# Up weights whose last 64 rows come as two loads of one column half each, with small loads moved in SyncE's order

## The chip, the core and the metric

The kernel runs on one core of one Trainium2 chip. The metric is the device time of one execution in microseconds (us). A profiled execution has a span of its own (first to last instruction) and a time of its own.

## The reference

Three stages follow one another; the result has 3072 rows of 320.

```python
# 1: mLSTM over 4 batches, 8 heads, 768 steps, head size 40
C = f_stab * C + i_stab * outer(v_t, k_t);  n = f_stab * n + i_stab * k_t
y_t = sigmoid(o_t) * (C @ q_t) / max(|n . q_t|, 1)
x = y.transpose(0, 2, 1, 3).reshape(3072, 320)
# 2: soft mixture of 8 experts, 4 slots each
logits = x @ phi                                  # phi: 320 x 32
slot_input = softmax(logits, 0).T @ x             # 32 x 320
slot_out[e] = relu(slot_input[e] @ w1[e]) @ w2[e] # w1: 320 x 1024, w2: 1024 x 320, 8 experts
x = softmax(logits, 1) @ slot_out
# 3: second mixture, weights w1, w2 of its own, gate 320 x 8
P = exp(x @ w_gate - max), then 8 rounds of row and column normalisation
out = sum over e of P[:, e:e+1] * (relu(x @ w1[e]) @ w2[e])
```

## The kernel before

**Stage 1** works through 24 chunks of 128 time steps (`NT` = 24). `step(i)` handles chunk i and prepares chunks i+1 and i+2; its parts are run in the order that the string `ORDER` (for i = 0: `ORDER0`) gives. The names that matter here: `KT`/`QT` transpose k and q of chunk i+2 on TensorE (`ptk`, L379); `E0`/`E1` compute the decay of chunk i+2 on TensorE (`pe`, L398) out of the rows `R`, which come from DRAM for two chunks at a time; `V` is `pv` (L473), the product with the values of chunk i. SyncE (SP) issues all loads but two, in program order, because TensorE, ScalarE, SP, VectorE and GpSimd follow the order written by hand in this part:

- `DK` (`load_kq`, L151) loads k and q of chunk i+5 into one of three buffers, `DV` (`load_v`, L156) the values of chunk i+2 into one of three, `O` (`load_o`, L161) the output gates some chunks ahead, each load of 128 rows of 8 pieces of 40 numbers.
- `R` (`load_R`, L334) loads the rows for two later chunks, in every second step.
- `W` (`load_w`, L672) takes the next `WN[i]` pieces of the weights of stage 2 from the generator `ahead_parts`.
- `load_small` loads `phi` (three loads) and the gate weights of stage 3 (`wg_sb`, three loads by `load_k`, L121), once, ahead of step 0. `lg_p` reads `phi_sb` first in step 5; `wg_sb` is read only after the last expert of stage 2.

`end()` does the last two chunks, in the order of `END`; its entry `sl20` sends what `ahead_parts` still has.

**Weights.** Every weight matrix has 320 x 1024 or 1024 x 320 numbers (1280 KB) and takes one slot in SBUF. There are 15 slots. Slots 0 to 10 are filled by `ahead_parts`; the others (`wb`) only after stage 1 has given its memory back, and the first ones are used again for the weights of the last expert and the first of stage 3. An up weight (`w1_parts`) is sent in pieces: two of 128 rows of 1024 numbers (512 KB each), and the last 64 rows, which lie in the slot as two blocks of 64 partitions, one for each half of the columns:

```python
yield v[:, 4, :], src[e, 256:320, :].rearrange("p (a f) -> a p f", a=2)
```

The destination of this piece is 128 partitions of 512 numbers; the source has the dimensions 2 (column half), 64 (row), 512 (column). A down weight (`w2_parts`) is sent in two pieces of 640 KB.

**Stage 2** runs expert by expert: `up_t(e)` transposes (`pth`, L1035), `up(e + 1)` multiplies with the up weight (`pu`, L1010 for the first 256 rows and L1016 for the last 64), `down(e)` with the down weight (`pd`, L1046). After the last expert, `s1_p(0)` multiplies with the first up weight of stage 3 (again `pu`, L1010 and L1016; its slot is `big`).

**Stage 3** is the long one: for each of 8 experts and 6 blocks of 512 rows, `g1` computes the hidden values (`z`, L1269) and `g2` the products (`y`, L1290 to L1292). Up weights of later experts are loaded by `load_m2w`, also through `w1_parts`.

Of the kernel before, what the change touches and what calls it, by code (L numbers as in the profile page):

```python
# [20 lines left out]
def mlstm_moe_kernel(  # L21
# [16 lines left out]
    nc = tc.nc  # L38
    B, H, S, D = q.shape
    N, DM = out.shape  # L40
    E, _, F = m2_w1.shape
# [9 lines left out]
    KT = [(0, 112), (112, 112), (224, 96)]  # L51
# [10 lines left out]
    NXR = 13  # L62
    NBIG = 3
    ORDER = (
        "LF' STm PK R DV O W CS E0 E0a E0g YC' Yg' KT KTa QT QTa X Xa E1 E1a E1g G0 DK LT LV I ST UM STd CB V US LP LD G LA S"
        " W0 W1 YB"
    )
    ORDER0 = "O KT KTa QT E0 E0a QTa E0g ST STd PC PK V E1 E1a E1g G0 DK CB DP US S W0 W1 YB"
# [50 lines left out]
    def load_k(eng, dst, src):  # L119
        for kt, (o, n) in enumerate(KS):  # L120
            eng.dma_start(out=dst[0:n, kt, :], in_=src[o:o + n, :])  # L121
# [31 lines left out]
    def load_v(i):  # L153
        b, c = divmod(i, NCH)
        sl = slice(c * L, (c + 1) * L)
        nc.sync.dma_start(out=vz[i % NV][:, :, 0:D], in_=v[b, :, sl, :].rearrange("h p d -> p h d"))  # L156

    def load_o(i0, i1):
        for i in range(i0, i1):
            b, c = divmod(i, NCH)  # L160
            nc.sync.dma_start(  # L161
                out=xs_(i).rearrange("p (h d) -> p h d", h=H),
                in_=o_gate[b, :, c * L:(c + 1) * L, :].rearrange("h p d -> p h d"),
            )
# [17 lines left out]
    O0 = 3  # L182
# [107 lines left out]
    def load_csa():  # L290
        for a in range(3):
            nc.sync.dma_start(
                out=csa[a * BH:(a + 1) * BH, :].rearrange("r (g s) -> r g s", g=SG),
                in_=cpd.rearrange("(g r) a s -> r g a s", g=SG)[:, :, a, :],
            )
# [35 lines left out]
    def load_R(p):  # L331
        b, c = divmod(p * CPS, NCH)
        r0 = c // CPS * BH + b * H
        nc.sync.dma_start(out=Rt[p % 2][96:99, :, :], in_=gpd[r0:r0 + H, :, :].rearrange("r a s -> a r s"))  # L334
# [21 lines left out]
    def load_small():  # L356
        for kt in range(NKT - 1):
            nc.sync.dma_start(out=phi_sb[:, kt, :], in_=phi[KT[kt][0]:KT[kt][0] + 112, :])
        nc.sync.dma_start(out=phi_sb[16:112, NKT - 1, :], in_=phi[224:320, :])
        load_k(nc.sync, wg_sb, m2_wg)  # L360

    Cst = [mid.tile([P, JP, D1], F32, name=f"C_{j}", bufs=1) for j in range(2)]
    Cbd = [mid.tile([P, JP, 2, D1], F32, name=f"Cb_{j}", bufs=1) for j in range(2)]
# [73 lines left out]
    def st_p(i):  # L437
        for j in range(JP):
            for r in range(2):
                nc.tensor.matmul(  # L440
                    o_c[DP * r:DP * r + D, j, :], kp[i % PD][:, 2 * j + r, :], vz[i % NV][:, 2 * j + r, :],
                    start=True, stop=True, tile_position=(0, DP * r),
                )

    def st_m(i):
        if i % NCH:
            Cds[i] = mid.tile([P, JP, D1], F32, tag="Cd", name="Cd")
            nc.gpsimd.tensor_tensor(
                out=Cds[i], in0=Cst[(i % NCH - 1) % 2], in1=dec[:, :, i:i + 1].to_broadcast([P, JP, D1]),
                op=ALU.mult,  # L450
            )

    def st_d(i):
        Cn = Cst[i % NCH % 2]
        if i % NCH:
            nc.vector.tensor_tensor(out=Cn, in0=o_c, in1=Cds.pop(i), op=ALU.add)
        else:
            nc.vector.tensor_copy(Cn, o_c)
# [199 lines left out]
    def w1_parts(dst, src, e):  # L658
        v = dst.rearrange("p (a f) -> p a f", f=F // 2)
        for t in range(2):  # L660
            yield v[:, 2 * t:2 * t + 2, :].rearrange("p a f -> p (a f)"), src[e, t * P:(t + 1) * P, :]
        yield v[:, 4, :], src[e, 256:320, :].rearrange("p (a f) -> a p f", a=2)

    def w2_parts(dst, src, e):
        v = dst.rearrange("p (k d) -> p k d", d=DM)
# [4 lines left out]
    def load_w(parts):  # L670
        for d, s_ in parts:
            nc.sync.dma_start(out=d, in_=s_)  # L672
# [26 lines left out]
    ahead_parts = ahead()  # L699

    def step(i):
        b, c = divmod(i, NCH)
        n, s1 = i + 2, i + 1
        T, S1 = n < NT, s1 < NT
        X = i >= 2
        gq, j = divmod(i - 2, 4)
        if j < 3:
            gq -= 1
        if gq < 0:
            j = 9  # L710
        C_ = c < NCH - 1
        nxt = b + 1 < B

        ops = dict(
            KT=lambda: T and k_p(n, 0), KTa=lambda: T and k_a(n, 0),
            QT=lambda: T and k_p(n, 1), QTa=lambda: T and k_a(n, 1),
            E0=lambda: T and e_p(n, 0), E0a=lambda: T and e_a(n, 0), E0g=lambda: T and e_g(n, 0),
            E1=lambda: T and e_p(n, 1), E1a=lambda: T and e_a(n, 1), E1g=lambda: T and e_g(n, 1),
            ST=lambda: C_ and st_p(i), STm=lambda: C_ and st_m(i), STd=lambda: C_ and st_d(i), CB=lambda: C_ and st_b(i),
            S=lambda: S1 and s_p(s1), W0=lambda: S1 and s_d(s1, 0), W1=lambda: S1 and s_d(s1, 1),  # L720
            PK=lambda: T and pr_k(n),
            V=lambda: pv(i), I=lambda: c and p_st(i),
            X=lambda: X and x_p(i - 2), Xa=lambda: X and x_a(i - 2),
            Yg=lambda: i in nqs and y_g(i),
            UM=lambda: c and y_u(i), US=lambda: y_a(i), YB=lambda: i < NT - 3 and y_b(i), YC=lambda: i in ysrc and y_c(i),
            G=lambda: i in SIG and sig_o(*SIG[i]),
            G0=lambda: i or sig_o(0, 1), PC=lambda: put_csl(1), DP=decays_p,
            CS=lambda: i % HC == 1 and i + 5 < NT and put_csl((i + 5) // HC),
            LT=lambda: j == 1 and lt_p(gq), LV=lambda: j == 1 and lt_v(gq),
            LP=lambda: j in (2, 3) and (sl_p, lg_p)[j - 2](gq),  # L730
            LD=lambda: j in (1, 2, 3) and (lt_d, sl_d, lg_d)[j - 1](gq),
            LA=lambda: j in (1, 3) and (lt_a, lg_e)[j // 2](gq),
            LF=lambda: j == 1 and lt_f(gq),
            O=lambda: load_o(*LO[i]),
            R=lambda: i and i % CPS == 0 and i + 4 < NT and load_R((i + 4) // CPS),
            W=lambda: load_w(islice(ahead_parts, WN[i])),
            DV=lambda: T and i and load_v(n),
            DK=lambda: i + 5 < NT and load_kq(i + 5),
        )
        for o in (ORDER if i else ORDER0).split():  # L740
            if o.endswith("'"):
                if last:
                    last[-1][o[:-1]]()
            else:
                ops[o]()
        last[:] = [ops]
# [19 lines left out]
    load_o(0, 1)  # L766
    load_R(1)
    load_v(2)
    load_csa()
    load_o(1, 2)  # L770
    e_g(0, 0)
    pr_k(0)
    e_g(0, 1)
# [10 lines left out]
    put_csl(0, SW)  # L784
    masks()
    decays_d()
    load_small()
    load_w(islice(ahead_parts, 1))
    load_o(2, O0)
    load_kq(4)  # L790
    load_R(2)
    load_o(O0, O0 + 1)
    load_w(islice(ahead_parts, 1))
    nc.gpsimd.memset(xr[:, :, DM:DM + 1], 1.0)
# [6 lines left out]
    SIG = {s: (s + 2, s + 3) for s in range(4, 22)} | {1: (1, 2), 2: (2, 4), 3: (4, 6)}  # L801
    OL = [4, 5, 6, 7] + list(range(8, NT)) + [NT] * NT
    LO = {i: (OL[i], OL[i + 1]) for i in range(NT + 1)}
    WN = [0, 1] * 8 + [1, 1, 2, 2, 3, 3]
    for i in range(NT - 2):
        step(i)
    def end():
        n0, n1, n2, n3 = range(NT - 4, NT)
        wide = lambda t: t.rearrange("p a l -> p (a l)")[:, 0:H * D1].rearrange("p (h d) -> p h d", h=H)
        ux, ov = {}, {}  # L810

        def own(key):
            ov[key] = wide(ps_s.tile([P, 4, L], F32, tag="s", name=key))
            return ov[key]

        def u_(i):
            ux[i] = wide(pre.tile([P, 4, L], F32, tag="dd", name="ux", bufs=6))
            u_m(i, ux[i], ov.get("st", o_st) if i == n3 else o_st)

        def r_(i):  # L820
            u_s(i, ux[i], ov["in"] if i == n3 else o_in)
            ysrc[i] = ux[i]

        todo = dict(
            st=lambda: (st_m(n2), st_p(n2)), sl20=lambda: load_w(ahead_parts), d20=lambda: (st_d(n2), st_b(n2)),
            s23=lambda: s_p(n3, ((ps_e, "e"), (ps_t, "t"))), w0=lambda: s_d(n3, 0), w1=lambda: s_d(n3, 1),
            lt4=lambda: lt_p(gl - 1), tv4=lambda: lt_v(gl - 1), q4=lambda: sl_p(gl - 1), e4=lambda: sl_d(gl - 1),
            i22=lambda: p_st(n2), v22=lambda: pv(n2), i23=lambda: p_st(n3, own("st")), v23=lambda: pv(n3, own("in")),
            y21=lambda: y_c(n1, nc.gpsimd), y22=lambda: y_c(n2, nc.gpsimd), y23=lambda: y_c(n3),
        )  # L830
        for j, i in enumerate((n0, n1, n2, n3)):
            todo[f"x{20 + j}"] = lambda i=i: x_p(i)
            todo[f"a{20 + j}"] = lambda i=i: x_a(i)
            todo[f"u{20 + j}"] = lambda i=i: u_(i)
            todo[f"r{20 + j}"] = lambda i=i: r_(i)
            todo[f"n{20 + j}"] = lambda i=i: y_b(i)
            todo[f"g{20 + j}"] = lambda i=i: y_g(i)
        for o in END.split():
            todo[o]()
# [662 lines left out]
```

## Time and profile before

| | us |
|---|---|
| median of 3 runs | 956.61 (955.43 to 956.73) |
| profiled execution, its own time | 954.06 |
| its span | 952.3 |
| TensorE busy in the span | 909.3 |
| VectorE / ScalarE / GpSimd busy | 571.0 / 359.0 / 95.3 |

TensorE is busy for 95% of the span. Of the chain of work that ended last, 89% of the span is TensorE and 7% DMA. The granted TensorE clock, as a mean over the span, is 0.976 of full speed. The span has three parts: stage 1 to about 156 us, stage 2 to about 219 us, stage 3 from there to the end.

### The profile page before, as it was taken

The page shows a single profiled execution, that of the slowest core. Times are in us where ns is not written, and L with a number is a line of the kernel's source. Part 1 is how long each engine was busy: PE and PEld are TensorE (multiplying, and loading weights), DVE is VectorE, ACT ScalarE, POOL GpSimd, SP SyncE. Part 2 cuts the span into 40 slices and gives each one's busy share as a digit, 9 for nine tenths or more (in the row PEclk, how much of TensorE's full clock was granted, in tenths as well). Part 3 has the DMA queues.
Part 4 walks back from the last instruction along what each step waited for, and adds up shares of the span by engine and source line. Part 5 has one row for each costly group of instructions (what it writes and reads, how often), then busy time and mean ns, then how long its engine had stood idle before and what let it go on. Part 6 is the DMA issues. An engine that isn't in the chain of part 4 may idle for free.

```text
span 952.3 us, 18828 instructions
## 1 busy us (share of the span) xinstructions
PE 909.3 (95%) x7972; PEld 628.9 (66%) x7972; DVE 571.0 (60%) x1168; ACT 359.0 (38%) x701; POOL 95.3 (10%) x194
## 2 busy tenths in 40 slices
PE   8799977858999999999999999999999999999998
PEld 5688865424667666666666666666666666666665
DVE  7477845614689768575557456645745565544543
ACT  6455642315334335243433244224424343423221
POOL 5566652000000000000000000000000000000000
PEclk9899987969999999999999999999999999999999
DMA  6898988864021003010101011001100000000111
GB/s 125 171 205 155 210 191 242 240 205 135 1 63 36 14 1 112 1 56 1 56 2 56 1 57 50 7 17 40 56 1 1 1 1 1 1 1 29 49 42 49
DMA packets 128973, 63.85 MB, mean 67 GB/s; under 512 B 102425, under 2 KB 122649, under 8 KB 128889
## 3 DMA queue, kind: packets, MB, share of 16 engines
q1 hardware_dynamic: 128617, 62.16, 25.3%
q8 instruction: 62, 1.02, 0.4%
q10 hardware_dynamic: 272, 0.49, 0.2%
q14 instruction: 22, 0.18, 0.1%
HBM read 58.20 MB, written 4.23 MB: 66 GB/s over the span
## 4 chain that ended last, share of the span: by engine, by line
PE 89%; DMA 7%; DVE 2%; SPq 1%; ACT 1%; issue 0%; POOL 0%; ACTq 0%; DVEq 0%
PE y L1290 22%; PE y L1292 22%; PE y L1291 22%; PE z L1269 9%; PE ptk L379 2%; PE pss L428 2%; PE oa L473 2%; DMA wb<-in_moe_w_dram 2%; DMA big<-in_moe_w_dram 2%; PE pe L398 1%; DMA kq<-in_k_dram 1%; PE ob L484 1%; DMA vz<-in_v_dram 1%; PE ptx L548 1%; DMA R<-gpd 1%; SPq L672 1%
## 5 line engine op out<-in xcount | busy, mean ns | idle before, releaser
L1290 PE MATMUL y<-wx,hh 128*128 128x320 f16 x1344 | 402.1, 299 | 0.0
L1292 PE MATMUL y<-wx,hl 128*128 128x320 f16 x1344 | 401.7, 299 | 0.0
L1291 PE MATMUL y<-wx,hh 128*128 128x320 f16 x1344 | 401.6, 299 | 0.0
L1272 ACT ACTIVATE hh<-z 128x512 f16<-128x512 f32 x384 | 209.4, 594 | 431.5 <-PE z L1269 430.9
L1273 DVE SCALAR_TENSOR_TENSOR hl<-z,hh 128x512 f16<-128x512 f32 x384 | 248.4, 686 | 52.9 <-ACT hh L1272 52.4
L1305 DVE SCALAR_TENSOR_TENSOR acc<-y,Ps,acc 128x320 f32<-128x320 f32 x168 | 92.4, 550 | 209.9 <-PE y L1292 209.5
L1290 PEld LDWEIGHTS <-hh 128*128 128x128 f16 x1536 | 150.5, 98 | 73.2 <-ACT hh L1272 0.5
L1291 PEld LDWEIGHTS <-hh 128*128 128x128 f16 x1536 | 150.4, 98 | 73.2
L1292 PEld LDWEIGHTS <-hl 128*128 128x128 f16 x1536 | 149.9, 98 | 60.6 <-DVE hl L1273 1.9
L1269 PE MATMUL z<-cst,sst 96*128 96x512 f16 x384 | 115.8, 380 | 1.3 <-DVE sst L1206 1.0
L1292 PE MATMUL y<-wh,hl 128*128 128x320 f16 x192 | 57.4, 299 | 0.3 <-DVE hl L1273 0.3
L1290 PE MATMUL y<-wh,hh 128*128 128x320 f16 x192 | 57.4, 299 | 0.0
L1291 PE MATMUL y<-wl,hh 128*128 128x320 f16 x192 | 57.3, 299 | 0.0
L1269 PEld LDWEIGHTS <-sst 96*128 96x128 f16 x384 | 37.4, 99 | 18.9 <-issue 2.9
L407 ACT ACTIVATE dd<-pe 128x512 f32<-128x512 f32 x48 | 29.2, 608 | 37.3 <-PE pe L398 37.0
L435 DVE TENSOR_TENSOR dd<-pss,dd 128x512 f32<-128x512 f32 x48 | 30.9, 686 | 14.9 <-PE pss L428 12.6
L379 PE MATMUL ptk<-ident,kq 128*128 128x128 f32 x192 | 28.2, 295 | 7.5 <-DMA kq<-in_k_dram 7.5
L1095 POOL PARTITION_ALL_REDUCE mr<-mx x8 | 3.0, 377 | 319.6 <-DVE mx L1084 318.5
L1095 POOL PARTITION_ALL_REDUCE mr<-mxs x8 | 2.9, 363 | 318.9 <-DVE mxs L1114 318.9
L412 POOL TENSOR_SCALAR_AFFINE_SELECT dd<-dd 128x512 f32<-128x512 f32 x48 | 30.6, 636 | 17.1 <-ACT dd L407 17.0
L379 PEld LDWEIGHTS ptk<-ident,kq 128*128 128x128 f32 x192 | 24.6, 152 | 10.4 <-issue 5.5
L428 PE MATMUL pss<-T,T 64*128 64x128 f32 x384 | 27.9, 285 | 0.0
(260 smaller groups left out, 719.1 us busy)
## 6 DMA issues: line engine op xcount, KB each, us to landing
wa<-in_moe_w_dram SPq DMA_DIRECT2D x18, 512.0 KB
raw<-in_moe_w_dram SPq DMA_DIRECT2D x28, 320.0 KB
kq<-in_k_dram SPq DMA_DIRECT2D x24, 160.0 KB
kq<-in_q_dram SPq DMA_DIRECT2D x24, 160.0 KB
vz<-in_v_dram SPq DMA_DIRECT2D x24, 160.0 KB
xr<-in_o_gate_dram SPq DMA_DIRECT2D x24, 160.0 KB
wb<-in_moe_w_dram SPq DMA_DIRECT2D x6, 640.0 KB
out_dram<-acc SPq DMA_DIRECT2D x24, 160.0 KB
```

The source lines that it names most:

```text
L379: nc.tensor.transpose(pt[:, j, :], kq[i % NQ][:, a, 2 * j:2 * j + 2, :].rearrange("p h d -> p (h d)"), ident,)
L407: nc.scalar.activation(out=dd, in_=tmp.pop(("e", i, hh)), func=AF.Exp)
L412: nc.gpsimd.affine_select(out=dd, in_=dd, pattern=[[0, 4], [1, L]], compare_op=ALU.is_ge, fill=0.0, base=0, channel_multiplier=-1,)
L428: nc.tensor.matmul(ps[r][:, j, :], Ts[i, 0][rs_, j, :], Ts[i, 1][rs_, j, :], start=True, stop=True, tile_position=(DP * r, 0),)
L435: nc.vector.tensor_tensor(out=dds[i, r], in0=tmp["s", i][r], in1=dds[i, r], op=ALU.mult)
L1269: nc.tensor.matmul(z, Sst[e][:, kc * P:(kc + 1) * P], cst[:, tb * TB:(tb + 1) * TB], start=True, stop=True,)
L1272: nc.scalar.activation(out=hh[:, kc, :], in_=z, func=AF.Relu)
L1273: nc.vector.scalar_tensor_tensor(out=hl[:, kc, :], in0=z, scalar=0.0, in1=hh[:, kc, :], op0=ALU.max, op1=ALU.subtract)
L1290: nc.tensor.matmul(y, hh[:, kc, ts], wh[e][:, kc, :], start=(kc == 0), stop=False)
L1291: nc.tensor.matmul(y, hh[:, kc, ts], wl[e][:, kc, :], start=False, stop=False)
L1292: nc.tensor.matmul(y, hl[:, kc, ts], wh[e][:, kc, :], start=False, stop=(kc == KF - 1))
L1305: nc.vector.scalar_tensor_tensor(out=a, in0=y, scalar=Ps[:, i, e:e + 1], in1=a, op0=ALU.mult, op1=ALU.add)
```

## The change

The last 64 rows of an up weight are now two loads, one for each column half, each of 64 rows of 512 numbers onto 64 partitions. As an up weight now has four pieces and not three, `WN` gives more pieces to the last six steps. `phi` is loaded in step 2 (`SM`, behind `DK`), the gate weights of stage 3 behind the last piece of `ahead_parts`. Of the early loads, the output gates of chunk 1 go ahead of `csa`, and the k and q of chunk 4 and the second `R` go ahead of the first weight piece and the output gates of chunk 2.

```diff
     ORDER = (
-        "LF' STm PK R DV O W CS E0 E0a E0g YC' Yg' KT KTa QT QTa X Xa E1 E1a E1g G0 DK LT LV I ST UM STd CB V US LP LD G LA S"
+        "LF' STm PK R DV O W CS E0 E0a E0g YC' Yg' KT KTa QT QTa X Xa E1 E1a E1g G0 DK SM LT LV I ST UM STd CB V US LP LD G LA S"
         " W0 W1 YB"
     )
@@ load_small
         nc.sync.dma_start(out=phi_sb[16:112, NKT - 1, :], in_=phi[224:320, :])
-        load_k(nc.sync, wg_sb, m2_wg)
@@ w1_parts
-        yield v[:, 4, :], src[e, 256:320, :].rearrange("p (a f) -> a p f", a=2)
+        for a in range(2):
+            yield v[64 * a:64 * a + 64, 4, :], src[e, 256:320, a * (F // 2):(a + 1) * (F // 2)]
@@ step
             W=lambda: load_w(islice(ahead_parts, WN[i])),
+            SM=lambda: i == 2 and load_small(),
@@ ahead of step 0
     load_v(2)
+    load_o(1, 2)
     load_csa()
-    load_o(1, 2)
@@
-    load_small()
-    load_w(islice(ahead_parts, 1))
-    load_o(2, O0)
     load_kq(4)
     load_R(2)
+    load_o(2, O0)
+    load_w(islice(ahead_parts, 1))
     load_o(O0, O0 + 1)
@@
-    WN = [0, 1] * 8 + [1, 1, 2, 2, 3, 3]
+    WN = [0, 1] * 8 + [2, 2, 2, 3, 3, 3]
@@ end
-            sl20=lambda: load_w(ahead_parts),
+            sl20=lambda: (load_w(ahead_parts), load_k(nc.sync, wg_sb, m2_wg)),
```

The order of the instructions on TensorE, ScalarE and GpSimd is the same in both kernels; on SP it differs. In the rows below, `-` stands for the kernel before and `+` for the changed one. SP ahead of step 0 (`kq` is a buffer of k and q, `R` the rows for the decay, `wa` a weight slot, `xr` output gates):

```order
-L358 DMA phi_sb<-in_moe_phi_dram 112x32 x2
-L359 DMA phi_sb<-in_moe_phi_dram 96x32
-L121 DMA wg_sb<-in_moe_w_gate_dram 128x8 x2
-L121 DMA wg_sb<-in_moe_w_gate_dram 64x8
-L672 DMA wa<-in_moe_w_dram 128x1024
-L161 DMA xr<-in_o_gate_dram 128x8x40
 L151 DMA kq_101<-in_k_dram 128x8x40
 L151 DMA kq_101<-in_q_dram 128x8x40
 L334 DMA R_118<-gpd 3x8x256
+L161 DMA xr<-in_o_gate_dram 128x8x40
+L672 DMA wa<-in_moe_w_dram 128x1024
 L161 DMA xr<-in_o_gate_dram 128x8x40
```

Eight loads that stood ahead of `R` are behind it now, or in a later step.

SP in step 1, ahead of the third load of `R`, which step 4 needs:

```order
 L161 DMA xr<-in_o_gate_dram 128x8x40
-L672 DMA wa<-in_moe_w_dram 128x1x512
+L672 DMA wa<-in_moe_w_dram 64x512
 L151 DMA kq_100<-in_k_dram 128x8x40
 L151 DMA kq_100<-in_q_dram 128x8x40
```

In the place of the piece with both column halves stands one half; the other one follows in step 3.

SP in steps 18 to 20 (`kq_102` is that of the last chunk, `bigx` two weight slots, `vz` values):

```order
-L672 DMA big<-in_moe_w_dram 128x1x512
-L672 DMA bigx<-in_moe_w_dram 128x4x320
+L672 DMA big<-in_moe_w_dram 64x512 x2
 L151 DMA kq_102<-in_k_dram 128x8x40
 L151 DMA kq_102<-in_q_dram 128x8x40
 L156 DMA vz_106<-in_v_dram 128x8x40
 L161 DMA xr<-in_o_gate_dram 128x8x40
-L672 DMA bigx<-in_moe_w_dram 128x4x320
+L672 DMA bigx<-in_moe_w_dram 128x4x320 x2
```

Ahead of the last k and q stand two halves instead of one piece with both and one down piece; that down piece has moved behind them.

## Rows read from the trace of the kernel before

**Rows 1.** The page: forty equal slices of the span, in tenths.
```profile
PE   8799977858999999999999999999999999999998
PEclk9899987969999999999999999999999999999999
DMA  6898988864021003010101011001100000000111
```

**Rows 2.** The chain that ended last, 20 to 220 us: start, us, what.
```profile
38.02 4.83 DMA R<-gpd
...
126.93 9.76 DMA kq<-in_k_dram
...
143.16 10.55 DMA vz<-in_v_dram
...
178.18 15.91 DMA wb<-in_moe_w_dram
...
202.50 15.65 DMA big<-in_moe_w_dram
```

**Rows 3.** DMA issues of the execution: kind, engine, count, KB each.
```profile
wa<-in_moe_w_dram SPq DMA_DIRECT2D x9, 256.0 KB
```

**Rows 4.** Stretches: last three columns are granted TensorE clock, DMA share, GB/s.
```profile
52.00:56.00 4.00, 4.00 (x82) 3.56 (x79) 2.62 (x6) 2.07 (x6) 2.25 (x4) 1.00 1.11 195
136.90:142.10 5.20, 5.20 (x56) 4.58 (x58) 0.38 (x1) 2.55 (x5) 2.56 (x4) 0.50 1.04 281
139.50:142.00 2.50, 2.50 (x43) 2.23 (x44) 0.28 (x1) 1.33 (x3) 0.63 (x1) 0.50 1.01 374
...
211.00:212.00 1.00, 0.92 (x17) 0.42 (x16) 0.55 (x1) 0.09 (x1) 0.00 (x0) 1.00 1.07 438
213.00:216.00 3.00, 2.54 (x28) 1.28 (x26) 0.56 (x4) 0.00 (x0) 0.00 (x0) 1.00 0.13 49
234.00:238.00 4.00, 4.00 (x30) 2.78 (x29) 2.46 (x5) 2.50 (x7) 0.00 (x0) 1.00 0.14 51
```

**Rows 5.** TensorE in order of time, stage 1: start, us, line, [idle before <-releaser].
```profile
28.36 0.39 PE L398 MATMUL pe<-R,csl 99*128 99x512 bf16 x1 [1.32 <-DMA R<-gpd]
...
42.90 0.61 PE L398 MATMUL pe<-R,csl 99*128 99x512 bf16 x1 [4.83 <-DMA R<-gpd]
...
136.83 1.94 PE L379 MATMUL ptk<-ident,kq 128*128 128x128 f32 x8 [5.07 <-DMA kq<-in_k_dram]
...
153.85 1.94 PE L473 MATMUL in<-vz,dd 128*64 128x41 f32 x32 [4.67 <-DMA vz<-in_v_dram]
```

**Rows 6.** Stretches by the first column, at half clock; second pair is TensorE busy.
```profile
42.90:46.50 3.60, 3.60 (x17) 2.83 (x19) 0.00 (x0) 2.38 (x5) 1.32 (x2) 0.50 1.19 208
...
155.80:162.50 6.70, 6.28 (x46) 3.27 (x47) 3.37 (x11) 2.02 (x4) 0.24 (x2) 0.50 0.94 274
172.80:176.20 3.40, 3.40 (x36) 1.30 (x24) 1.21 (x5) 0.69 (x2) 0.00 (x0) 0.50 0.97 235
```

**Rows 7.** TensorE in order of time, stage 2.
```profile
185.80 0.44 PE L1035 MATMUL pth<-ident,h 128*128 128x128 f32 x2
...
189.58 0.44 PE L1035 MATMUL pth<-ident,h 128*128 128x128 f32 x2
...
206.92 1.08 PE L1016 MATMUL pu<-wa,siT 128*32 128x256 f32 x8 [5.88 <-DMA wa<-in_moe_w_dram]
...
210.07 0.56 PE L1035 MATMUL pth<-ident,h 128*128 128x128 f32 x2
...
214.47 1.07 PE L1010 MATMUL pu<-big,soT 128*32 128x256 f32 x16
218.29 0.75 PE L1016 MATMUL pu<-big,soT 128*32 128x256 f32 x8 [2.75 <-DMA big<-in_moe_w_dram]
```

**Rows 8.** SP in order of time: issues.
```profile
19.71 2.22 SPq L121 DMA_DIRECT2D wg_sb<-in_moe_w_gate_dram  x3
...
33.81 4.12 SPq L151 DMA_DIRECT2D kq<-in_q_dram  x1
```

More of the change, by code (lines that the diff above doesn't have):

```diff
@@ L824, in end @@
         todo = dict(
-            st=lambda: (st_m(n2), st_p(n2)), sl20=lambda: load_w(ahead_parts), d20=lambda: (st_d(n2), st_b(n2)),
+            st=lambda: (st_m(n2), st_p(n2)), sl20=lambda: (load_w(ahead_parts), load_k(nc.sync, wg_sb, m2_wg)), d20=lambda: (st_d(n2), st_b(n2)),
             s23=lambda: s_p(n3, ((ps_e, "e"), (ps_t, "t"))), w0=lambda: s_d(n3, 0), w1=lambda: s_d(n3, 1),
```

## Prediction

> **What bounds the kernel now.** I read the page's slices first [rows 1]: TensorE is full from the eleventh slice on (from about 238 us), so stage 3 runs at TensorE's pace and takes over every microsecond won ahead of it. The holes are in slice 2 and in slices 6 to 10: TensorE at 5 to 8 tenths, its clock below full in most of them, DMA at 4 to 8 tenths. Then the chain that ended last [rows 2]: up to 220 us it leaves TensorE for five long DMA pieces, each a load that took 5 to 16 us. SP's order shows what they have in common: the two longest, 15.91 and 15.65 us, are the loads of 128 partitions x 512 numbers with the column half as the source's outermost dimension, and the R, kq and vz loads were issued a few places behind one of these.
>
> The stretches say why [rows 4]. While only such a load is left, DMA moves 49 GB/s at a share of 0.13 of 16 engines, which is two engines of 16 (0.125); 234 to 238 us shows the same again (0.14, 51 GB/s). With wide loads only, share 1.01 to 1.07, it moves 374 and 438 GB/s. So a piece of 256 KB [rows 3] is carried by two engines at about 24.5 GB/s each: 131,072 bytes by 24.5 GB/s is 5.35 us on each of the two, while fourteen have nothing of it to do. Everything behind it that also has a share on those two engines lands late. It also blocks SP: the q load issued just behind the first such piece took 4.12 us to issue [rows 8], and R, next in line, came that much later.
>
> **Part 1: the last 64 rows as two loads.** Price of a half (131,072 bytes): no row has a wide load onto 64 partitions, so I bound it: 5.35 us if one engine carries it alone, 0.30 us at 438 GB/s. I take 0.35 us, at 374 GB/s, because a half now begins with 64 rows on both sides, as the loads that run on all engines begin with 128. On this the page "DMA: Bandwidth & Descriptors" of the Trainium skill has a rule (section on why a DMA increments its semaphore by 16): a load uses the largest number of engines up to 16 that divides the slowest dimension of both sides, which makes 2 of the old piece and 16 of a half. The 0.13 of the trace agrees for the old piece; no run here shows the other yet.
>
> A rule speaks against it: "SBUF — State Buffer", section "Door 1: The DMA port swizzle", says that 64 partitions reach half of the ports, with 196 GB/s measured against 328 for 128 partitions. By it a half costs 0.67 us, an estimate from that page, and the 14 halves from step 18 to the end of stage 2 cost 4.5 us more than mine; that takes half of the slack worked out below and would not by itself move the end.
>
> What TensorE loses now, and what I let go, by place:
> - R for step 2: 1.32 us idle [rows 5]; goes by part 2.
> - R for step 4: 4.83 us idle [rows 5], behind the first two-engine piece. It goes. The idle brought the clock to 0.50 (1.2 of 2.4 GHz), and 3.60 us of full work ran at that [rows 6]: half, 1.8 us, comes back.
> - k of the last chunk: 5.07 us idle [rows 5], then 5.20 us of full work at 0.50 [rows 4]: 2.6 us back.
> - v of the last chunk: 4.67 us idle, and the 1.94 us product behind it at half clock [rows 5]: 0.97 us back.
> - The end of stage 1: 6.28 us of work at 0.50 in 6.7 us [rows 6]. At full clock 3.1 us of it would go; VectorE's steps lie between, so I take 2.3.
> - Stage 2: from one expert's transpose to the next it takes 3.78 us where nothing is late (185.80 to 189.58, [rows 7]). The next two take 20.49 us, to 210.07: 20.49 - 2 x 3.78 = 12.9 us go. From 210.07 to 214.47 stays. The second half of the first product of stage 3 starts 3.82 us behind the first half, at 218.29, and needs some 0.9: 2.9 go.
>
> Sum: 1.3 + 4.8 + 1.8 + 5.1 + 2.6 + 4.7 + 1.0 + 2.3 + 12.9 + 2.9 = 39.4 us.
>
> What is late next? The loads must keep ahead of that faster TensorE. At the issue of the last k (126.93 us, [rows 2]) the changed order still has 13 weights of 1,310,720 bytes to send, 17.0 MB, and six loads of 163,840 bytes. At 374 GB/s the weights take 45.6 us; the six, at the 195 GB/s of a stretch of such loads [rows 4], 5.0 us. TensorE is 7.9 us earlier there (1.3 + 4.8 + 1.8), so from 119 us the last byte lands near 170 us; it is wanted at 218.29 - 39.4 = 178.9 us. Nine microseconds of slack; at the mixed rate of 281 GB/s [rows 4] the weights take 60.6 us and it lands 6 us late. The last k and v have less ahead of them than before: k two halves (0.7 us) in place of 5.35 us on two engines and a 640 KB piece.
>
> **Part 2: order and small loads.** Eight loads leave R's way. The three gate-weight loads alone hold SP 2.22 us [rows 8], more than the 1.32 us that TensorE waits; so that wait goes, and step 4's R starts earlier too. The three phi loads at step 2 have three steps until their first reader; the gate weights land behind slot 10, with all of stage 2 as cover. Were that cover gone, each set costs its 2.2 us of issue once. I price them at nothing. The same for k and q of chunk 4, only earlier.
>
> **Part 3: WN.** Steps 1 to 15 send one weight less, steps 16 to 21 more. What that crowds is the last k and v; a return of all of their waits costs 5.07 + 2.6 + 4.67 + 0.97 = 13.3 us. Cover: the 5.35 us pieces that made them late are gone. The 16 additional issues cost at 0.74 us each (2.22 / 3) no more than 11.8 us of SP over the whole run and nothing where it waits for TensorE anyway.
>
> **The sum** is made against the profiled execution (954.06 us, 2.55 below the median): 954.06 - 39.4 = 914.7. Against the median of the runs: 956.61 - 39.4 = 917.2 us, my number. If the clock does not fall at 172.8 us, 1.7 us more come back [rows 6].
>
> **Rivals.**
> 1. *Loads still end last, for lack of rate.* For it: 281 GB/s where kinds mix, no row that shows a load onto 64 partitions, denser pieces in steps 16 to 21. Against: 374 and 438 GB/s [rows 4]. Price: 6 us at 281 GB/s (923 us), or 13.3 us if the last k and v are late as before (930 us).
> 2. *The change does not spread the piece*: each half still runs on two engines, the same 5.35 us of two engines per weight. Then only the order gains, 1.3 to 3 us: 954 to 955 us. Against: nothing in a half has a dimension of 2 any more.
> 3. *Slower: each half runs on one engine, and both on the same one.* Then that engine carries 262,144 bytes per up weight, 10.7 us and not 5.35, seven times from step 18 to the end of stage 2: 7 x 5.35 = 37 us on the chain that already ends last, less 1.3: 992 us. It decides once a half takes over about 5.4 us. For it: the two column halves ran on two engines, one each as it seems. Against: the loads that begin with 128 rows use all.
>
> **How the numbers follow.** Forecast 0.63, by itself 911 to 922 us; rival 1 0.27; rival 2 0.05; rival 3 0.03; anything else 0.02. The range 908 to 931 us takes in forecast and rival 1 with their bounds. About 0.2% (1.9 us) is what a measurement here can tell from no change. Faster: 0.63 + 0.27 + most of rival 2's 0.05, 0.94. Same: 0.03. Slower: rival 3, 0.03.
>
> **What would show it.** In the profile of the changed kernel: no 256 KB issue, twice as many of 128 KB; no stretch at share 0.13 with 49 GB/s; TensorE's waits for R (1.32, 4.83), kq (5.07) and vz (4.67) gone, and with them the 0.5 clock at 40 and 137 us; experts about 3.8 us apart to the last; the span near 913 us, all of the gain made before stage 3 begins near 180 us. I am wrong if the chain still leaves TensorE for weight loads of stage 2 (rival 1), if the 0.13 stretches stay (rival 2), or if a stretch at a share near 0.06 appears (rival 3).

## The result and the profile after

The changed kernel takes 921.25 us (median of 6 runs, 920.35 to 921.54), the kernel before 956.67 us on the same chip (6 runs, 954.25 to 959.1): ratio 0.963, with a 95% interval of 0.9614 to 0.9645. Forecast: 917.2 us, range 908 to 931. The profiled execution took 920.35 us, with a span of 918.6 us; its granted clock is 0.996 as a mean (before: 0.976).

The page of the changed kernel: busy time of the engines, three rows of forty slices, and the chain that ended last by engine; the last row is one kind of DMA issue (count, KB each, median us to landing).

```profile
PE 896.8 (98%) x7972; PEld 624.0 (68%) x7972; DVE 572.0 (62%) x1168; ACT 358.8 (39%) x701; POOL 95.4 (10%) x194
...
PE   8999977999999999999999999999999999999998
...
PEclk9999989999999999999999999999999999999999
DMA  8999999840200030101010101010100000001111
...
PE 93%; DVE 2%; DMA 2%; SPq 1%; ACT 1%; issue 0%; POOL 0%; ACTq 0%; POOLq 0%; DVEq 0%
...
wa<-in_moe_w_dram SPq DMA_DIRECT2D x18, 128.0 KB, 4.5
```

Against [rows 1], TensorE is full from slice 8 on and not from slice 11, the clock is below nine tenths in one slice only, and the DMA row is at 9 tenths in slices 2 to 7. DMA has 2% of the chain where it had 7%. The nine issues of 256 KB [rows 3] are now eighteen of 128 KB. The engines of a load can be counted, as the trace records a landing for each: the first old piece, issued at 32.60 us in the kernel before, has two (41.36 and 41.40 us), a half, issued at 172.59 us in the changed kernel, has sixteen (174.97 to 175.17 us).

TensorE in order of time in the changed kernel, with the wait ahead of an instruction in brackets:

```profile
118.00 0.39 PE L397 MATMUL pe<-R,csl 99*128 99x512 bf16 x1 [0.45 <-DMA R<-gpd]
...
135.13 0.78 PE L439 MATMUL ob<-vz,kp 128*40 128x41 f32 x16 [5.75 <-DMA vz<-in_v_dram]
...
141.39 1.08 PE L472 MATMUL in<-vz,dd 128*64 128x41 f32 x32
142.40 0.54 PE L547 MATMUL ptx<-ident,xr 128*112 128x128 f32 x3
...
154.34 1.07 PE L1010 MATMUL pu<-wa,siT 128*32 128x256 f32 x16
...
167.10 0.44 PE L1035 MATMUL pth<-ident,h 128*128 128x128 f32 x2
...
169.98 0.44 PE L1035 MATMUL pth<-ident,h 128*128 128x128 f32 x2
...
184.67 0.61 PE L1016 MATMUL pu<-big,soT 128*32 128x256 f32 x8
```

The four waits of [rows 5] are gone, and so are those of [rows 7]: no instruction of stage 2 waits for a weight. It is close, though: the last piece of the weight in the last row landed at 184.34 us, 0.33 us ahead of the product. One long wait is new, 5.75 us for the values of chunk 22. The last product of stage 1 (`in`, the `V` of the last chunk) starts at 141.39 us and not 153.85; the second half of the first product of stage 3 at 184.67 us and not 218.29 [rows 7]. From there on both kernels need the same: 952.3 - 218.29 = 734.0 us and 918.6 - 184.67 = 733.9 us. All of the gain is made ahead of stage 3.

SP, which issues the loads, around that new wait, and then what SP itself waited for from 150 to 180 us (total, times, longest):

```profile
123.50 1.67 SPq L672 DMA_DIRECT2D bigx<-in_moe_w_dram  x3
125.27 0.61 SPq L156 DMA_DIRECT2D vz<-in_v_dram  x1
125.92 3.57 SPq L672 DMA_DIRECT2D bigx<-in_moe_w_dram  x3
```
```profile
SPq L672 <- DMA cst<-cst: 9.5, 1, 9.5
```

The late values were issued at 125.27 us, right behind three weight pieces, and TensorE got them at 135.13. The last of these rows is a stand of 9.5 us: SP waited for a transfer that ScalarE had issued (`cst`, constants of stage 3), although its own next load (a weight) doesn't touch `cst`. Two pieces of that weight had gone into the same slot at 161.41 and 162.77 us. What joins the two is a semaphore: in the trace `cst` and the waiting load signal the same one, and the load was issued at 172.59 us, right behind the last landing of `cst` at 172.57.

Stretches of the changed kernel (first pair: length, TensorE busy; last three columns: granted clock, DMA share, GB/s):

```profile
130.00:140.00 10.00, 4.87 (x59) 4.27 (x59) 2.77 (x8) 1.17 (x4) 0.64 (x2) 0.66 1.11 304
140.00:150.00 10.00, 7.66 (x134) 5.01 (x130) 6.60 (x20) 3.15 (x8) 3.50 (x8) 1.00 1.06 334
...
172.00:174.00 2.00, 1.47 (x18) 0.62 (x18) 1.00 (x2) 1.48 (x4) 0.00 (x0) 1.00 0.08 8
```

From 140 to 150 us all 16 engines are busy (1.06), on weights but for three small loads of the gate weights, and move 334 GB/s, not the 374 of [rows 4]. Around 173 us, behind SP's stand, DMA had run dry.

### The profile page after: what moved, and what is told of

The parts are those of the page before. It is cut to its first block, busy times and chain, and to the rows that moved or that the text cites. A ratio compares the mean times of both kernels' runs of the same rounds, so it can differ in the third digit from the quotient of the medians.

```text
span 918.6 us, 18865 instructions
## 1 busy us (share of the span) xinstructions
PE 896.8 (98%) x7972; PEld 624.0 (68%) x7972; DVE 572.0 (62%) x1168; ACT 358.8 (39%) x701; POOL 95.4 (10%) x194
## 4 chain that ended last, share of the span: by engine, by line
PE 93%; DVE 2%; DMA 2%; SPq 1%; ACT 1%; issue 0%; POOL 0%; ACTq 0%; POOLq 0%; DVEq 0%
PE y L1290 22%; PE y L1292 22%; PE y L1291 22%; PE z L1269 9%; PE pss L427 2%; PE ptk L378 2%; PE oa L472 2%; PE pu L1010 2%; PE pe L397 1%; SPq L672 1%; PE ob L483 1%; PE pd L1046 1%; DMA bigy<-in_moe_w_dram 1%; PE ptx L547 1%; PE pu L1016 1%; PE ob L312 1%
## 5 line engine op out<-in xcount | busy, mean ns | idle before, releaser
L427 PEld LDWEIGHTS pss<-T,T 64*128 64x128 f32 x384 | 24.1, 193 | 4.6 <-issue 3.9
```

Source lines behind the costliest of these rows:

```text
L427: nc.tensor.matmul(ps[r][:, j, :], Ts[i, 0][rs_, j, :], Ts[i, 1][rs_, j, :], start=True, stop=True, tile_position=(DP * r, 0),)
```

## The experiments

Two questions: what made the gain (spread of the piece, or order), and where the 4 us to the forecast stayed. Ratios are to the kernel before, run on the same chip.

### Split or order

The kernel before with the two halves alone, then the changed kernel with the old piece and the old `WN`:

```diff
-        yield v[:, 4, :], src[e, 256:320, :].rearrange("p (a f) -> a p f", a=2)
+        for a in range(2):
+            yield v[64 * a:64 * a + 64, 4, :], src[e, 256:320, a * (F // 2):(a + 1) * (F // 2)]
```

> The kernel before with the two half loads alone; order of the early loads, phi, gate weights and WN as before. Theory S (the number of DMA engines that carry the last 64 rows makes the gain): nearly all of it stays, 920 to 928 us; TensorE still waits 1.3 us for the second R, no longer 4.8 us for the third; no stretch at a DMA share of 0.13. Rival O (the order of the early loads and the small loads made it): 945 us or more. Rival N (two loads of half the size, between which others pass): as S.

922.04 us, ratio 0.9643 (0.9622 to 0.9664): a time that can't be told from that of the changed kernel. Its waits are others: 1.07 us for R of step 2, 2.44 us for the values of the last chunk and, in stage 2, 2.78 us for weights (0.41, 1.84, 0.32, 0.21), where the changed kernel has 5.75 us for the values of chunk 22 and none for weights.

> The changed kernel with the last 64 rows in one load again, column half outermost, and WN as before; the order of the early loads and the late small loads stay. Theory S: 949 to 956 us, the waits for R in step 4 (4.8 us), kq (5 us), vz (4.7 us) and for the weights of stage 2 are back; only the 1.3 us of the second R are gone. Rival O: 921 to 930 us. Rival N: as S.

955.26 us, ratio 0.9986 (0.997 to 1.0002). TensorE's waits in that kernel:

```profile
40.27 0.39 PE L397 MATMUL pe<-R,csl 99*128 99x512 bf16 x1 [3.23 <-DMA R<-gpd]
...
134.39 1.94 PE L378 MATMUL ptk<-ident,kq 128*128 128x128 f32 x8 [4.39 <-DMA kq<-in_k_dram]
...
151.04 1.94 PE L472 MATMUL in<-vz,dd 128*64 128x41 f32 x32 [4.29 <-DMA vz<-in_v_dram]
```

The old piece alone brings three of the four waits of [rows 5] back, whatever the order; only the 1.32 us for R of step 2 stays gone. Order and small loads win 1.4 us (0.0014 of the time), with an interval from nothing to 2.9 us: it can't be told from no change.

### How many engines

The changed kernel with its two halves, but the 64 rows of a half rearranged so that the source's outermost dimension is 2, then 4:

```diff
-            yield v[64 * a:64 * a + 64, 4, :], src[e, 256:320, a * (F // 2):(a + 1) * (F // 2)]
+            yield v[64 * a:64 * a + 64, 4, :], src[e, 256:320, a * (F // 2):(a + 1) * (F // 2)].rearrange(
+                "(p b) f -> b p f", b=2
+            )
```

> The changed kernel, but each half takes its 64 rows in two interleaved sets of 32, so that the source's outermost dimension is 2 again. Same loads, sizes and order as the changed kernel; the rows of these blocks meet other rows of the left operand, so the sums of the products leave the reference. Theory S: the two-engine stretches (share 0.13, 49 GB/s) are back, 948 to 962 us. Rival N (number and size of the loads count, not the engines): 919 to 924 us. Rival O: 919 to 924 us.

953.79 us, ratio 0.9964 (0.9949 to 0.9978).

> As the run with sets of 32, but four interleaved sets of 16 rows, outermost dimension 4 (again other rows meet in these blocks). Theory S with the engines given by that dimension: a half is on four engines, 32 KB each, 1.3 us at 24.5 GB/s, so both halves cost 2.7 us on four engines in place of 5.35 us on two: 922 to 935 us, and stretches at a share near 0.25 if any. If only dimension 2 is special: as the changed kernel, 919 to 924 us. Rival N: 919 to 924 us.

933.97 us, ratio 0.9761 (0.9737 to 0.9786). This is the median of two runs. A stretch of each in which hardly anything but such loads is left, outermost 2 first:

```profile
214.00:218.00 4.00, 1.89 (x23) 0.73 (x22) 0.51 (x3) 0.00 (x0) 0.00 (x0) 1.00 0.13 50
```
```profile
208.00:209.00 1.00, 1.00 (x8) 0.67 (x7) 0.52 (x2) 0.60 (x1) 0.35 (x1) 1.00 0.26 100
```

Two engines of 16 at 50 GB/s, four at 100 GB/s: the outermost dimension sets the number of engines, 25 GB/s each. The time follows it, 953.8, 934.0 and 921.25 us for 2, 4 and 64. That the piece now comes as two smaller loads makes little of the gain: with two loads on two engines 3.4 us of it are left (0.36% of the time), and the changed order is in that rest too.

### Where the 4 us stayed: the late values

First suspect: the 5.75 us wait. This kernel takes the three pieces of step 19 away from ahead of the values of chunk 22.

```diff
-    WN = [0, 1] * 8 + [2, 2, 2, 3, 3, 3]
+    WN = [0, 1] * 8 + [2, 2, 2, 0, 3, 3]
```

> The changed kernel with WN 2, 2, 2, 0, 3, 3 in the last six steps, so that no weight piece stands ahead of the values of chunk 22. Theory V (the 4 us by which the gain fell short are the wait for these values, 5.75 us, and the half clock behind it): the wait is gone, stage 1 ends 6 to 8 us earlier, and so does the kernel: 913 to 916 us. Theory Q (the weights of stage 2 now land just in time, so DMA's total sets the end of stage 2): the wait is gone or smaller, stage 1 ends earlier, stage 2 waits for weights by as much: 918 to 923 us.

921.38 us, ratio 0.9623 (0.9595 to 0.965). TensorE:

```profile
134.66 1.13 PE L472 MATMUL in<-vz,dd 128*64 128x41 f32 x32 [1.01 <-DMA vz<-in_v_dram]
...
172.71 0.64 PE L1010 MATMUL pu<-wa,siT 128*32 128x256 f32 x8 [3.00 <-DMA wa<-in_moe_w_dram]
...
186.02 0.75 PE L1016 MATMUL pu<-big,soT 128*32 128x256 f32 x8 [0.79 <-DMA big<-in_moe_w_dram]
```

Stage 1 ends 6.7 us earlier, and all of it is given back: 5.6 us of waiting for weights in all, the last of them in use at 186.02 us, 1.35 us later than in the changed kernel. The loads of the weights set the end; the late values only hid it. Whether their rate does or SP's stand, this run can't say: SP stands 8.2 us for `cst` here too.

So the next kernels send weights earlier (`WN` = [0,2] + [0,1] x 4 + [0,2] + [0,1] x 2 + [1,1,2,1,1,3]), take ScalarE's transfer out of SP's way, and then do both:

```diff
-        nc.scalar.dma_start(out=cst[32:64, :], in_=cst[0:32, :])
+        nc.gpsimd.tensor_copy(cst[32:64, :], cst[0:32, :])
```

(With this edit the copy is also written behind `pow2_w(0)` and no longer ahead of it.)

> The changed kernel with the weights spread otherwise: both halves of a weight in one step (steps 1 and 11), four weights done by step 15 (three in the changed kernel), then 1, 1, 2, 1, 1, 3 pieces. Theory V: no wait for values, 912 to 915 us. Theory Q: the 1.3 MB more by step 15 are some 4 us of DMA less later; the end of stage 2 still waits for loads, 916 to 920 us. Against both: a wait for R or kq in steps 2 to 15 that the changed kernel has not, 921 us or more.

920.38 us, ratio 0.9621 (0.9598 to 0.9644): a little over the 916 to 920 us of theory Q. No values are waited for; R at 48.46 us is (1.47 us), and weights of stage 2 are (3.4 us in all).

> The changed kernel with that copy alone on GpSimd. Both theories: TensorE had every weight of stage 2 just in time, so the time stays, 919 to 922 us, while the last weight of stage 2 (the first up weight of stage 3) lands 3 to 4 us earlier than at 184.3 us.

919.63 us, ratio 0.961 (0.9582 to 0.9639): the time is as expected, but the last weight landed at 182.80 us, 1.5 us earlier and not 3 to 4. In its profiled execution the wait for the values of chunk 22 is 3.56 us, with the same stage 1: that wait differs from one execution to the next.

> As the run with weights early, and the copy of 32 rows of cst made by GpSimd in place of a DMA of ScalarE's queue, whose semaphore a weight load of SP waits for (SP stood still 162.8 to 172.6 us in the changed kernel, DMA at a share of 0.08 in 172 to 174 us). Theory Q: 2 to 4 us under the run with weights early, 913 to 917 us. Theory V: as that run.

918.15 us, ratio 0.96 (0.9578 to 0.9622): 2.2 us under the run with weights early, as expected, but over the 913 to 917 us. Waits of stage 2 in this last kernel, the pieces of the chain that ended last behind which they stand, and its stretch of weights:

```profile
172.80 0.64 PE L1010 MATMUL pu<-wa,siT 128*32 128x256 f32 x8 [0.77 <-DMA wa<-in_moe_w_dram]
...
182.26 0.80 PE L1016 MATMUL pu<-big,soT 128*32 128x256 f32 x8 [0.59 <-DMA big<-in_moe_w_dram]
```
```profile
161.32 11.44 DMA wa<-in_moe_w_dram
172.78 9.24 DMA big<-in_moe_w_dram
```
```profile
140.00:150.00 10.00, 7.19 (x77) 3.83 (x65) 6.16 (x18) 3.46 (x12) 0.00 (x0) 1.00 1.06 330
```

> The kernel of 918.15 us with another spread of the weight pieces alone: WN = [0,1] x 6 + [2,1,1,1,1,2,1,1,1,3], in place of [0,2] + [0,1] x 4 + [0,2] + [0,1] x 2 + [1,1,2,1,1,3]. Theory that the total of the weights' transfer sets the end of stage 2 and the spread only decides which small load waits: the wait for R at 47.58 us (0.91) goes with the second piece of step 1, the last weight lands near 182 us as before, 916.5 to 918.5 us. If the pieces in steps 12 to 21 crowd k and v again: a wait of 1 us or more for kq or vz and 919 us or above, as in the changed kernel itself.

919.03 us, ratio 0.96 (0.9584 to 0.9616): not to be told from the kernel of 918.15 us, and 0.5 us over the time expected. The wait for R is gone and the last weight is in use at 181.61 us, as expected; no wait for kq or vz reaches 1 us. The four kernels lie within 2.3 us of one another, with overlapping intervals. In the three with the copy on GpSimd SP no longer waits for `cst`, and from about 160 us to the last up weight the chain that ended last runs through loads of weights alone. Neither their place nor SP is the limit there, but their rate, the 330 GB/s.

### The price of a half

The same kernel (918.15 us) with the last 64 rows as one load onto all 128 partitions, which also begins with 128 on both sides. With `WN` counted accordingly it has sent the same four weights by step 15.

```diff
-        for a in range(2):
-            yield v[64 * a:64 * a + 64, 4, :], src[e, 256:320, a * (F // 2):(a + 1) * (F // 2)]
+        yield v[:, 4, :], src[e, 256:320, :].rearrange("r (a f) -> (r a) f", a=2)
```

> The kernel of 918.15 us (weights early, the conversion constants copied on GpSimd), with the last 64 rows of an up weight sent as ONE load onto all 128 partitions (rows and column halves interleaved, 128 rows of 512 numbers on both sides), where it had two loads onto 64 partitions each; WN counts pieces accordingly. The rows of these weights meet other rows of the input, so the sums leave the reference; the work and its order do not. What it tells: the price of a half. If a load onto 64 partitions runs at the same rate as one onto 128 (my 0.35 us, 374 GB/s), the bytes and their time are unchanged: 917 to 919.5 us, waits of stage 2 for weights as in that kernel (0.77, 0.40, 0.59 us, each within 1 us). If it runs at about half the rate (0.67 us, the rule weighed in the prediction), 14 halves from step 18 on give back 14 x 0.32 = 4.5 us of transfer: the last weight lands 3 to 4.5 us earlier than 182.0 us, the waits for weights in stage 2 vanish, and the time falls by what those waits are, 1.8 us or a little more: 914.5 to 916.8 us.

914.11 us, ratio 0.9555 (0.9541 to 0.9569): far from the 917 to 919.5 us of the same rate, a little under the other range. Its stretch of weights, and the product for which TensorE waited 0.59 us:

```profile
140.00:150.00 10.00, 6.83 (x64) 3.66 (x63) 6.24 (x19) 3.66 (x11) 0.00 (x0) 1.00 1.06 372
```
```profile
177.03 0.61 PE L1015 MATMUL pu<-big,soT 128*32 128x256 f32 x8
```

The same bytes, the same share of 1.06, 372 GB/s in place of 330. No wait for weights is left; the product starts 5.2 us earlier. The three waits for weights were 1.76 us of that (0.77, 0.40, 0.59); part of the rest is TensorE's clock, granted at 0.66 from 150 to 155 us in the kernel of 918.15 us and at 1.00 here. An up and a down weight (2,621,440 bytes) take 7.05 us at 372 and 7.94 us at 330 GB/s: 0.89 us for two halves. A half so costs 0.35 + 0.45 = 0.80 us, an estimate from one stretch of 10 us (160 to 170 us, 382 against 342 GB/s, gives 0.75).

The records of single DMA packets say where that time goes. From 140 to 150 us a packet of 2,048 bytes, of which the last 64 rows are made, took 127 ns as a mean with two loads and 86 ns with one; a packet of 1,280 bytes, of a down weight, 71 and 60 ns. So it isn't a gap between two loads: the packets themselves take longer, and those of other weights beside them. On two engines there is no such difference: from 150 to 220 us a packet of 2,048 bytes took 104 ns in the kernel before (one load onto 128 partitions) and 102 ns with outermost dimension 2 (two loads onto 64).

And in the changed kernel itself, with this edit and a `WN` that ends on [1,1,2,2,3,3]. As an up weight again has three pieces, this sends a fourth weight by step 15 (the changed kernel: three) and two pieces, not three, in step 19:

> The changed kernel itself (921.25 us; its order, its loads of small weights, ScalarE's DMA for the constants) with one thing different: the last 64 rows as ONE load onto all 128 partitions, rows and halves interleaved; WN counts pieces as before. The rows meet other rows of the input, so the sums leave the reference. What it tells: how much of the 4 us between my 917.2 and 921.25 is the price of a load onto 64 partitions. If that price is the missing term (0.35 us taken, some 0.8 us paid in a full queue: 14 halves, 6 us of transfer): the wait of 5.75 us for the values of chunk 22 shrinks by the two halves sent ahead of it, the weights of stage 2 come earlier, and the time falls to 915 to 918.5 us. If the missing 4 us are SyncE's stand behind ScalarE's DMA and the order of step 19 alone: the time stays within 2 us of 921.25.

916.43 us, ratio 0.9579 (0.9555 to 0.9603); the interval doesn't touch that of the changed kernel. TensorE and the stretch:

```profile
129.75 0.51 PE L439 MATMUL ob<-vz,kp 128*40 128x41 f32 x16 [0.58 <-DMA vz<-in_v_dram]
...
134.82 1.13 PE L472 MATMUL in<-vz,dd 128*64 128x41 f32 x32 [0.56 <-DVE nq L514]
...
179.40 0.61 PE L1015 MATMUL pu<-big,soT 128*32 128x256 f32 x8
```
```profile
140.00:150.00 10.00, 7.56 (x87) 4.19 (x81) 6.07 (x18) 3.59 (x10) 0.00 (x0) 1.00 1.06 371
```

371 GB/s against 334 is 7.07 against 7.85 us for an up and a down weight, 0.39 us a half: 0.74 us in all. The wait for the values falls from 5.75 to 0.58 us, and the product at the end of stage 2 starts at 179.40 us; the prediction wanted it at 178.9. SP still stands 9.3 us here for ScalarE's transfer, and no load is waited for in stage 2. What isn't separated: of the 5.17 us at the values, a part may be order, since two pieces and not three go ahead of them here, and one weight more has gone by step 15. The closer pair is with the kernel of 920.38 us, which has also sent four weights by step 15, ends stage 1 as early (last product at 134.44 us, here 134.82) and stands 8.5 us for `cst`, but has the halves. Its product at the end of stage 2:

```profile
183.48 0.61 PE L1016 MATMUL pu<-big,soT 128*32 128x256 f32 x8
```

That is 4.1 us later than 179.40, and the medians are 4.0 us apart (920.38 and 916.43), as in the pair above (918.15 and 914.11). The two kernels here ran on two chips; the intervals of their ratios just touch (0.9598 and 0.9603), those of the pair above don't.

### A version that beats both

The kernel of 914.11 us with its readers laid out as the load is. A VectorE copy doubles the last 64 columns, one transposing product replaces two, and a parity mask (`par`) the two copies onto 64 partitions, so that rows and column halves meet as in the reference again. Left out below: the making of `par`, the same mask where `soT` is written, the third load of the gate weights, which goes onto every second partition, and the product that reads it.

```diff
+        nc.vector.tensor_copy(
+            dup.rearrange("p (r a) -> p r a", a=2), src[:, 2 * P:DM].unsqueeze(2).to_broadcast([P, DM - 2 * P, 2])
+        )
...
-        for a in range(2):
-            nc.tensor.matmul(
-                dst[64 * a:64 * a + 64, 2 * NS:3 * NS], src[:, 2 * P:DM], w, start=True, stop=True,
-                tile_position=(0, 64 * a),
-            )
+        nc.tensor.matmul(dst[:, 2 * NS:3 * NS], dup, w, start=True, stop=True)
...
-        for a, o in enumerate(halves(siT)[1:]):
-            ps_ = slice(64 * a, 64 * a + 64)
-            nc.vector.tensor_tensor(out=o, in0=ptf[ps_, 2 * NS:3 * NS], in1=rs[ps_, 0, :], op=ALU.mult)
+        for a in range(2):
+            nc.vector.scalar_tensor_tensor(
+                out=siT[:, 2 + a, :], in0=ptf[:, 2 * NS:3 * NS], scalar=par[:, a:a + 1], in1=rs[:, 0, :],
+                op0=ALU.mult, op1=ALU.mult,
+            )
```

> The kernel of 914.11 us, with the reader laid out as the load is: the last 64 columns of the slot inputs are doubled by one VectorE copy (128 partitions x 128 numbers) ahead of fold_t, one transposing product replaces two, and a parity mask takes the place of the two 64-partition copies, so that rows and column halves meet as they lie; the third gate-weight load goes onto every second partition. Theory that the bytes alone ran faster there and nothing else: two copies more on VectorE's path between the stages, at most 0.5 us each, so 914 to 915.5 us, no TensorE wait for weights in stage 2, last up weight of stage 2 near 174.4 us. Rival, that the layout brings something of its own back (the doubled copy delays the first product of stage 2 and of stage 3 each by over 1 us): 916 us or more.

912.91 us, ratio 0.9546 (0.9524 to 0.9567). The added copy, on VectorE:

```profile
145.19 0.23 DVE L902 COPY dup<-sacc 128x128 f32<-128x128 f32 x1
```

It takes 0.23 us, and TensorE waits for no weight in stage 2. 912.91 us is a little under the 914 to 915.5 us expected, but its runs (912.37 to 914.95) overlap those of the kernel above (913.67 to 915.3): the layout costs nothing that these runs can tell.

## Why the prediction was right, and where 4 us stayed

The mechanism held: two engines carried the old piece, 16 carry a half, and the waits behind it went. By place, with the profiled executions (952.3 and 918.6 us of span, 33.7 apart, 5.7 less than the 39.4 forecast; the medians are 35.4 apart, 4.0 less):

| Term | forecast | found |
|---|---|---|
| stage 1, R to the last v | 21.3 | 13.4 (155.79 to 142.40) |
| end of stage 1 to the first product of stage 2 | 2.3 | 0.75 (12.69 to 11.94) |
| stage 2 | 15.8 | 19.5 (49.81 to 30.33) |

(Before, the product behind the last v started at 155.79 us and the first of stage 2 at 168.48.)

That the sum misses by no more than this is in part luck: 3.7 us that stage 2 gave over its forecast stand against 9.5 us that the other two rows lack.

**Stage 1.** Each of the four waits went, as priced, and the clock stayed full behind them. What took 7.9 us away again is a wait of the same kind one chunk earlier: 5.75 us for the values of chunk 22, 0.45 us for R, and about 1.7 us of work at half clock behind it (0.66 as a mean from 130 to 140 us). The place is that of this execution; in the kernel with step 19 empty the same time is lost in stage 2.

**The step that failed** is the price of a half, "I take 0.35 us". It measured 0.74 to 0.80 us. The rows behind my 374 GB/s were loads onto 128 partitions, and I took a load's outermost dimension for all that sets its rate. The rule that I weighed against it (the Trainium skill, "SBUF — State Buffer", section "Door 1: The DMA port swizzle") came nearer with its 0.67 us; the trace agrees with it in direction and goes further. I also wrote that this price "takes half of the slack worked out below and would not by itself move the end". It moved the end by some 4 us: 4.0 in each of the two pairs above (918.15 to 914.11, 920.38 to 916.43), and 4.8 from the changed kernel itself (921.25 to 916.43), where order may have a part. At the 334 GB/s that the trace shows, the 13 weights take 51.0 us and not 45.6, so 5.4 us of the nine were gone; the last byte landed at 184.34 us and not "near 170". That the queue, full for longer, also held up the small loads between the weights is argued, not shown by itself. "The last k and v have less ahead of them" was true of k and false one chunk earlier, where v has three pieces right ahead of it.

**The slack** also left out that SP can stand. It stood 9.5 us, DMA ran dry, and the weights came just in time. But in the kernel of 916.43 us it stands as long, and nothing in stage 2 waits for a load; and taking the stand away alone gave 919.63 us, with overlapping intervals. So this is a second use of the slack, not the cause.

**The tail** brought 0.75 of 2.3 us: VectorE's steps set that stretch, and a faster TensorE waits for them. The rows that show it are one product's wait, in the kernel before and in the changed one, and the step in front of it in the chain of the changed kernel. The wait is put down to `mxg`, which this product doesn't read; the chain has VectorE's `xr` there, which it does:

```profile
159.08 0.86 PE L548 MATMUL ptx<-ident,xr 128*112 128x128 f32 x3 [0.42 <-DVE mxg L1145]
...
145.80 0.51 PE L547 MATMUL ptx<-ident,xr 128*112 128x128 f32 x3 [1.61 <-DVE mxg L1145]
```
```profile
145.17 0.48 DVE xr L536
```

**Stage 2** gave 3.7 us more than forecast. The clock didn't fall at 173 us (1.7 us, which I had named as open), and experts that wait for nothing are 2.88 us apart (167.10 to 169.98), not the 3.78 us that I took from [rows 7]. That distance has a wait of 0.69 us for ScalarE in it (`hT`), and recurs in the changed kernel at the same expert (169.98 to 173.75). Two such differences are 1.8 us.

**Order and small loads**, priced at 1.3 us plus part of a wait, can't be told from nothing (1.4 us, up to 2.9). Of the rivals, the first (rate) was the live one, and the result lies between it and the forecast, nearer to its 923 us than to 917.2. Its sign as I had named it, waits for weights in stage 2, wasn't there in the changed kernel; the loss sat at the values. The kernel with step 19 empty showed the loads of weights behind it, and those without SP's stand that it was their rate. Rivals 2 and 3 fall: a half has sixteen landings, no stretch of loads at 0.13 with 49 GB/s is left, and the run with outermost dimension 2 shows what the second would have cost (953.79 us).

## What to carry to other kernels

Look for stretches in which DMA is busy at a small fixed share (0.13, 0.26) while something waits: here it was a load with a small outermost dimension, and everything queued behind it came late. Reorder the access so that a large dimension is outermost, and land it on all 128 partitions: the first was worth 35 us here, the second some 4. When a wait goes and the time stays, look whether the queue behind it is full before moving loads about: five kernels that only moved or freed loads lay between 918.15 and 921.38 us.

## What the runs showed of the hardware

- The number of DMA engines of a load follows its outermost dimension: 2 gives a share of 0.13 and 50 GB/s, 4 gives 0.26 and 100 GB/s, and with 64 a load has sixteen landings. The rule of the Trainium skill ("DMA: Bandwidth & Descriptors", section on why a DMA increments its semaphore by 16) says so, and the trace agrees.
- Two engines move 49 to 50 GB/s onto 64 partitions a load (the run with outermost 2) as onto 128 [rows 4]. With all 16 at work the load onto 64 partitions is dearer: 0.74 to 0.80 us and not 0.35, at a DMA share that reads 1.06 in both. A full share doesn't mean full rate: packets of 2,048 bytes took 127 ns there and 86 ns onto 128 partitions. That the cost lies in the partitions and not in there being two loads follows from the packets' own times, and from the two loads on two engines, whose packets take no longer than those of one; two loads onto 128 partitions each, on 16 engines, were not tried.
- SP stood 9.5 us for a transfer of another engine's queue, which signals the same semaphore as its own next load and shares no data with it. With that transfer made a GpSimd copy, the stand was gone.
